# Reordering the loads at the start, moving eight rows of a transform into the prologue, and halving a pair of sums, in a fused Fourier-filter and feed-forward kernel on one core

## The chip, the core and the metric

The kernel runs on one core of a Trainium2 chip. The core has five engines with a program of their own each: TensorE (PE), VectorE (DVE), ScalarE (ACT), GpSimd (POOL) and SyncE (SP). Each takes its instructions strictly in the order written; an instruction that has to wait holds up all that stand behind it on that engine. Transfers between the chip's main memory and the on-chip memories are issued by SP, ACT or POOL and then run on 16 DMA engines that all three share. The metric is the time of one execution on the device, in microseconds (us).

## What is computed

```python
X = np.fft.rfft(x, axis=1)                       # x: 8 batches, 3008 tokens, 256 channels
Y = X * (filt_r + 1j * filt_i)[None, :, :]
y = np.fft.irfft(Y, n=3008, axis=1)
h = y.reshape(24064, 256) @ w_in                 # w_in: 256 x 2048
out = (h - np.tanh(h)) @ w_out                   # w_out: 2048 x 256
```

All inputs and the output are float32 except the weights, which arrive as 64-bit words and are converted to float32 on the core.

## The kernel before

The Fourier transform over 3008 = 64 x 47 tokens is done as matrix products in two stages each way. Tokens are taken in rows r of 47, of which r and 47 - r go together, so that 24 row pairs remain. For each batch there is a *first* stage (a product over the 64 tokens of a row, result to the scratch tensor `ct1`), a middle stage (over the rows, with the filter between there and back, result to the scratch tensor `ct2`), and a *last* stage (`last(i, z)`, from `ct2` through the tile `e2` to the tokens `ut` of a group of four row pairs). A group then goes through the feed-forward part in four units (`up`, `shrink`, `down`).

Batch 0 has to pass the whole transform before anything else can start. This is the **prologue**, some 80 us long: its first stage (`first0`, three chunks of eight rows, tiles `x0`, with the matrix `f0` that VectorE doubles out of the loaded half `fh`), transposes (`across`), the middle stage by seven groups of frequencies (`there0`, `filtered`, `back0`), reads of `ct2` into `e2` (`rest`), and `last(0)`. Where TensorE has nothing to do, `warmer(n)` issues n products whose result nobody reads; each stands as two rows in the trace, since a float32 product is done in two passes.

In the prologue's shadow two other things are done: the weights are converted (`converted`, five VectorE steps for each piece, and sums of pieces, `sums`, which only the later units need), and rows 0 to 7 of batch 1's first stage are computed (`first1`). The rest of batch 1's first stage, and batch 2's, is the generator `first(2, ...)`: one job is four rows of one batch, and jobs are placed between the units of the first groups at positions `due`. The first group's units use a plain form (`up_plain`, L719), the second group's first units already the form with the seven sums (`up`, L648).

The order on each engine is the order in which the code is written (`tc.manual_schedule()`); waits between engines come from the tile framework. Two of its habits matter here. A tile that takes over the space of another waits until everybody has done with the other; so the first tiles of the pool `dn`, opened after the prologue, wait for all users of the prologue's pool `pro` that lie in the same place. And every DMA counts on one of eight semaphores in turn, eight for SP and ACT together and eight for POOL; a DMA waits until the one that had its semaphore before has landed.

Names in the profile: `x`, `fh`, `f` are the tokens and the matrix of the first stage, `pf` its products in PSUM; `ct<-e` are writes of the middle stage's result, `e<-ct` the reads for `last`; `pu` the products of `last`, `odd` the copy of one of its two banks, `ut` the sum and the difference of the two banks; `raw`, `top`, `low`, `wu`, `wd` the steps of converting weights.

Of the kernel before, what the change touches and what calls it, by code (L numbers as in the profile page):

```python
# [9 lines left out]
F32 = mybir.dt.float32  # L10
I32 = mybir.dt.int32
I64 = mybir.dt.int64
# [3 lines left out]
ALU = mybir.AluOpType  # L16
# [101 lines left out]
def kernel(  # L118
# [27 lines left out]
    def dram(t, off, dims):  # L146
        return bass.AP(tensor=t, offset=off, ap=[list(d) for d in dims])
# [112 lines left out]
            for u in dict(after).get(k, ()):  # L260
                yield from sums(u)

    def load_x(t, b, r, n):

        nc.sync.dma_start(t[0:64, 0:n, :], dram(x.tensor, (b * SEQ + r) * DM,
                                                [[NR * DM, 64], [1, n * DM]]))
        lo = 1 if r == 0 else 0
        if lo:
            nc.sync.dma_start(t[64:128, 0, :], dram(x.tensor, b * SEQ * DM,
                                                    [[NR * DM, 64], [1, DM]]))  # L270
        nc.sync.dma_start(t[64:128, lo:n, :], dram(x.tensor, (b * SEQ + NR - r - lo) * DM,
                                                   [[NR * DM, 64], [-DM, n - lo], [1, DM]]))
        return t

    rows = slice(0, 64), slice(64, 128)
# [308 lines left out]
    def last(i, z, held=False):  # L584

        b, c = groups[i]
        n = sum(widths(c))
        e2, gt = e2s.pop(i)
        ut = dn.tile([128, 2, CH * 128], F32, tag="ut", bufs=2, name="ut")
        banks = z("pu", [128, 2, CH, 64])  # L590
        for h in range(2):
            for j, r in enumerate(order(c)):
                for bank, half in zip(banks, rows):
                    for m, part in enumerate(rows):
                        nc.tensor.matmul(bank[part, h, j],  # L595
                                         e2[half, r - CH * c, h * 128 + 64 * m:h * 128 + 64 * m + 64],
                                         gt[half, r - CH * c], start=True, stop=True)
        even, odd = banks
        for k in (1, 0) if held else (1,):
            t = tr.tile([128, 2, CH, 64], F32, tag="e1", bufs=2, name=("even", "odd")[k])  # L600
            ACT.copy(t, banks[k])
            even, odd = (even, t) if k else (t, odd)
        u4 = ut.rearrange("p h (j n) -> p h j n", n=128)
        m = sum(w == 128 for w in widths(c))
        V.tensor_add(u4[:, :, :, 0:64], even, odd)
        V.tensor_sub(u4[:, :, 0:m, 127:63:-1], even[:, :, 0:m], odd[:, :, 0:m])
        w = n // 2
        if i == 0:
            uts[i] = (ut, None, w)
            yield  # L610
            return
# [420 lines left out]
    with tc.tile_pool(name="tr", bufs=2) as tr, tc.manual_schedule():  # L1032
# [16 lines left out]
        with tc.tile_pool(name="pro", bufs=1) as pro, \  # L1049
# [118 lines left out]
            for half in range(2):  # L1168
                V.memset(sgn[64 * half:64 * half + 64], 1.0 - 2 * half)
            V.memset(filt[2][:, 0], 1.0)  # L1170
            xs, began = [], []
            for c in range(3):
                lo = int(c == 0)
                xt = big([128, 8, DM], F32, "x0")
                xs.append(xt)
                fh = pro.tile([128, 8, 64], F32, tag="e1", bufs=4, name="fh")
                (ACT if c else nc.sync).dma_start(fh, f_d[:, 512 * c:512 * c + 512])
                if lo:
                    V.memset(xt[64:128, 0], 0.0)
                for k in (0, 4):  # L1180
                    nc.sync.dma_start(xt[0:64, k:k + 4], dram(x.tensor, (8 * c + k) * DM,
                                                              [[NR * DM, 64], [1, 4 * DM]]))
                    at = max(k, lo)
                    (ACT if c + k == 0 else G).dma_start(
                        xt[64:128, at:k + 4], dram(x.tensor, (NR - 8 * c - at) * DM,
                                                   [[NR * DM, 64], [-DM, k + 4 - at], [1, DM]]))
                r = 8 * c
                V.tensor_copy(f0[:, r:r + 8, 0:64], fh)
                V.tensor_scalar(out=f0[:, r:r + 8, 64:128], in0=fh,
                                scalar1=sgn, scalar2=None, op0=ALU.mult)  # L1190
# [3 lines left out]
            for t in filt:  # L1194
                G.memset(t[0:SG, 2:4], 0.0)
            gate = cst.tile([1, 1], F32, name="gate")
            G.tensor_copy(gate, xs[2][64:65, 0, 0:1])
# [21 lines left out]

            first0(2)  # L1220

            def first1(x1):

                for r in range(0, 8, 2):
                    pf = z0("pf", [128, 2, DM])
                    for k in range(2):
                        nc.tensor.matmul(pf[:, k], f0[:, r + k], x1[:, r + k],
                                         start=True, stop=True)
                    if r % 4 == 0:
                        two = (tr.tile([128, 2, 2, DM], F32, tag="a1", bufs=1, name="a1") if r else  # L1230
                               buffer("xy").rearrange("p (m n) c -> p m n c", m=2))
                    a1 = two[:, r // 2 % 2]
                    ACT.copy(a1, pf)
                    nc.sync.dma_start(
                        dram(ct1[1], r * DM, [[NH * DM, 128], [1, 2 * DM]]), a1)
                    yield

            a2 = {0: across(0)}
            convert(5)
# [68 lines left out]
            next(late)  # L1308
            warmer(8)

        with tc.tile_pool(name="dn", bufs=2) as dn, \
                tc.tile_pool(name="ps", bufs=1, space=bass.MemoryType.PSUM) as ps:
# [57 lines left out]
            for _ in last(0, z2):  # L1370
                pass
            warm = psl([128, 256], "o3")
            for _ in range(4):
                nc.tensor.matmul(warm[0:KM], mats[:, 3 * KM:4 * KM], mats[:, 3 * KM:3 * KM + 256],
                                 start=True, stop=True)
# [147 lines left out]
```

## Time and profile before

| | |
|---|---|
| time, median of 3 runs | 2543.22 us (2541.65 to 2544.98) |
| the profiled execution's own time | 2542.18 us |
| its span in the trace | 2540.3 us |
| busy: PE, DVE, ACT, POOL | 2522.6, 1935.6, 1694.2, 1532.0 us |
| TensorE's granted clock | 0.999 |

Times in the trace are counted from the start of the span. A row of a timeline has the start, the time from the first start to the last end, the engine, the line of the program, what is written and read, the count, and in brackets how long the engine had been idle before and who ended that. "q" behind an engine's name is its sequencer: issuing a DMA, not doing it.

### The profile page before, as it was taken

The page shows a single profiled execution, that of the slowest core. Times are in us where ns is not written, and L with a number is a line of the kernel's source. Part 1 is how long each engine was busy: PE and PEld are TensorE (multiplying, and loading weights), DVE is VectorE, ACT ScalarE, POOL GpSimd, SP SyncE. Part 2 cuts the span into 40 slices and gives each one's busy share as a digit, 9 for nine tenths or more (in the row PEclk, how much of TensorE's full clock was granted, in tenths as well). Part 3 has the DMA queues.
Part 4 walks back from the last instruction along what each step waited for, and adds up shares of the span by engine and source line. Part 5 has one row for each costly group of instructions (what it writes and reads, how often), then busy time and mean ns, then how long its engine had stood idle before and what let it go on. Part 6 is the DMA issues. An engine that isn't in the chain of part 4 may idle for free.

```text
span 2540.3 us, 44575 instructions
## 1 busy us (share of the span) xinstructions
PE 2522.6 (99%) x17072; PEld 2173.1 (86%) x17072; DVE 1935.6 (76%) x2270; ACT 1694.2 (67%) x2551; POOL 1532.0 (60%) x1112
## 2 busy tenths in 40 slices
PE   9999999999999999999999999999999999999998
PEld 8678889888898888988888888898889888898887
DVE  6888877988678876888669886698866888555555
ACT  4666666667666766676667666666666666666665
POOL 5255665667556765676656665666655666455552
PEclk9999999999999999999999999999999999999999
DMA  9854224422343323342334322343123322110110
GB/s 245 261 150 117 65 54 100 112 65 53 86 108 91 82 69 89 80 112 59 80 87 105 87 56 72 96 111 89 36 72 84 92 66 53 26 31 19 25 22 19
DMA packets 333664, 211.37 MB, mean 83 GB/s; under 512 B 231645, under 2 KB 305531, under 8 KB 329793
## 3 DMA queue, kind: packets, MB, share of 16 engines
q1 hardware_dynamic: 319091, 184.93, 29.8%
q0 software_dynamic: 11120, 16.16, 2.3%
q10 hardware_dynamic: 3230, 7.34, 0.9%
q8 instruction: 136, 2.23, 0.4%
q14 instruction: 87, 0.71, 0.1%
HBM read 127.81 MB, written 83.39 MB: 83 GB/s over the span
## 4 chain that ended last, share of the span: by engine, by line
PE 96%; DVE 2%; DMA 1%; issue 0%; POOL 0%; ACT 0%; ACTq 0%; SPq 0%; POOLq 0%; DVEq 0%
PE o L821 44%; PE x L648 25%; PE z L648 12%; PE y L648 6%; PE pm L415 2%; PE pu L595 2%; PE pm L351 1%; PE o L883 1%; PE pf L308 1%; DMA filt<-in_filt_r_dram 1%; DMA x<-in_x_dram 0%; DMA ct<-e 0%; PE o L719 0%; PE x L719 0%; PE z L719 0%
## 5 line engine op out<-in xcount | busy, mean ns | idle before, releaser
L821 PE MATMUL o<-t,wd 128*128 128x256 f32 (+1 forms) x3008 | 762.7, 376 | 0.0
L619 POOL TENSOR_TENSOR t<-h 128x512 f32<-128x512 f32 (+1 forms) x184 | 303.6, 1650 | 707.3 <-DVE h L771 642.2
L771 DVE TENSOR_TENSOR h<-h,y 128x1024 f32<-128x1024 f32 (+1 forms) x384 | 571.0, 1487 | 156.4 <-ACT y L767 156.4
L821 PEld LDWEIGHTS o<-t,wd 128*128 128x128 f32 x3008 | 568.8, 190 | 84.5 <-POOL o L853 15.1
L648 PE MATMUL x<-tu,wu 128*128 128x256 f32 (+1 forms) x2256 | 571.4, 376 | 0.0
L821 PE MATMUL o<-h,wd 128*128 128x256 f32 (+1 forms) x2256 | 569.9, 375 | 0.2 <-DVE h L771 0.2
L648 PEld LDWEIGHTS x<-tu,wu 128*128 128x128 f32 x2256 | 427.4, 190 | 53.8 <-issue 3.9
L821 PEld LDWEIGHTS o<-h,wd 128*128 128x128 f32 x2256 | 428.3, 190 | 50.9 <-issue 0.8
L654 ACT COPY s<-x 128x512 f32<-128x512 f32 (+1 forms) x188 | 109.3, 581 | 517.4 <-PE x L648 517.3
L764 ACT ACTIVATE y<-y 128x1024 f32<-128x1024 f32 (+1 forms) x384 | 399.5, 1040 | 12.1
L767 ACT ACTIVATE y<-y 128x1024 f32<-128x1024 f32 (+1 forms) x384 | 399.8, 1041 | 4.6
L761 ACT ACTIVATE y<-h 128x1024 f32<-128x1024 f32 (+1 forms) x384 | 400.6, 1043 | 2.5 <-DVE h L697 1.7
L622 POOL TENSOR_TENSOR t<-h,t 128x512 f32<-128x512 f32 (+1 forms) x184 | 338.3, 1838 | 0.0
L620 POOL TENSOR_TENSOR t<-h,t 128x512 f32<-128x512 f32 (+1 forms) x184 | 310.5, 1688 | 14.4
L621 POOL TENSOR_TENSOR t<-h 128x512 f32<-128x512 f32 (+1 forms) x184 | 276.9, 1505 | 0.0
L654 ACT COPY u<-x 128x512 f32<-128x512 f32 (+1 forms) x376 | 214.1, 569 | 72.9 <-PE x L648 69.6
L697 DVE COPY h<-x 128x512 f32<-128x512 f32 (+1 forms) x188 | 127.6, 679 | 129.1 <-PE x L648 128.9
L689 DVE TENSOR_TENSOR h<-z,u 128x512 f32<-128x512 f32 (+1 forms) x188 | 127.2, 677 | 88.9 <-ACT u L654 88.5
L648 PE MATMUL x<-ut,wu 128*128 128x256 f32 (+1 forms) x752 | 194.0, 380 | 0.2 <-DVE h L697 0.2
L648 PE MATMUL z<-tu,wu 128*128 128x256 f32 (+1 forms) x752 | 190.2, 375 | 1.4 <-DVE h L705 1.4
L648 PE MATMUL y<-ut,wu 128*128 128x256 f32 (+1 forms) x752 | 190.1, 375 | 0.0
L648 PE MATMUL z<-ut,wu 128*128 128x256 f32 (+1 forms) x752 | 190.0, 375 | 0.0
(215 smaller groups left out, 2933.5 us busy)
## 6 DMA issues: line engine op xcount, KB each, us to landing
ft<-filt SPq DMA_DIRECT2D x28, 1024.0 KB
ct<-nn SPq DMA_DIRECT2D x56, 512.0 KB
e<-ct SPq DMA_DIRECT2D x47, 512.0 KB
a<-ct SPq DMA_DIRECT2D x112, 192.0 KB
out_dram<-ot SPq DMA_DIRECT2D x1248, 16.0 KB
x_sb<-in_x_dram SPq DMA_DIRECT2D x110, 128.0 KB
ct<-a SPq DMA_DIRECT2D x60, 128.0 KB
ct<-x_sb SPq DMA_DIRECT2D x60, 128.0 KB
```

Of the source, the lines that this page charges most:

```text
L619: by.tensor_sub(t[0], b[0][1], b[0][0])
L620: by.tensor_sub(t[1], b[1][1], t[0])
L621: by.tensor_sub(t[2], b[1][1], b[0][1])
L622: by.tensor_sub(t[3], b[1][0], t[1])
L648: nc.tensor.matmul(bank[:, k], wu[:, q - 1, (2 * u + k) * 128:(2 * u + k + 1) * 128], rhs[q - 1], start=(first and k == 0), stop=True, ski ...
L654: ACT.copy(t, X)
L697: V.tensor_copy(h[:, 2, :, 0:w], X)
L761: ACT.activation(y[k], ht[k], AF.Arctan, scale=TURN)
L764: ACT.activation(y[k], y[k], AF.Tanh, scale=BEND)
L767: ACT.activation(y[k], y[k], AF.Square, scale=SCALE, accum_out=y_sums[:, 2 * U + k // 2:2 * U + k // 2 + 1])
L771: V.tensor_mul(ht[k], ht[k], y[k])
L821: nc.tensor.matmul(product(q), wd[:, q - 1, (2 * u + k) * 128: (2 * u + k + 1) * 128], rhs[q - 1][:, k], start=(u == 0 and k == 0 and q == ...
```

## The change

Seven edits, in the order of the program.

1. The chunks of `x0` and `f` are issued in another order and from other queues. The first half of `f`'s first chunk goes ahead on SP; ACT carries the first chunk's upper tokens, the other half of that `f`, and then both later chunks of `f`; POOL carries the upper tokens of chunks 1 and 2 alone, and behind its memsets. `f0` is doubled in pieces of 4, 4, 8 and 8 rows. POOL's filter loads wait for the last of the upper tokens.
2. `warmer(15)` at the start becomes `warmer(8)`.
3. Rows 8 to 15 of batch 1's first stage leave `first(2, ...)` (two jobs fewer there) and come into the prologue, as a second `first1` with a tile `x1b`, which POOL loads. Its results go through two tiles that take the places of `raw` in the pool `pro`.
4. The results of both `first1` are written to `ct1` from POOL, 512 KB at a time, where SP wrote 256 KB at a time.
5. The reads of `ct2` for `last(0)`: those of the first five groups go to POOL's queue (`rest` of 25 rows), those of the last two (7 rows) to SP and ACT. The final conversions of the prologue and `first1` stand ahead of the latter.
6. `warmer(8)` at the end of the prologue becomes `warmer(2)`, and four products behind `last(0)` become two.
7. `last(0)` copies, adds and subtracts the two halves of its channels one after the other, where one operation took both.

```diff
@@ last(i, z)
+        if i == 0:
+            t = tr.tile([128, 2, CH, 64], F32, tag="e1", bufs=2, name="odd")
+            for h in range(2):
+                ACT.copy(t[:, h], odd[:, h])
+                V.tensor_add(u4[:, h, :, 0:64], even[:, h], t[:, h])
+                V.tensor_sub(u4[:, h, 0:m, 127:63:-1], even[:, h, 0:m], t[:, h, 0:m])
...
@@ the prologue's loads
-            for c in range(3):
-                (ACT if c else nc.sync).dma_start(fh, f_d[:, 512 * c:512 * c + 512])
-                for k in (0, 4):
-                    nc.sync.dma_start(xt[0:64, k:k + 4], ...
-                    (ACT if c + k == 0 else G).dma_start(xt[64:128, at:k + 4], ...
...
+            load_f(0, 0, 4, nc.sync)
+            load_high(0, 0, ACT)
+            load_low(0, 0, nc.sync)
+            load_f(0, 4, 4, ACT)
+            load_high(0, 4, ACT)
+            load_low(0, 4, nc.sync)
+            for c in (1, 2):
+                load_f(c, 0, 8, ACT)
+            for c in (1, 2):
+                for k in (0, 4):
+                    load_low(c, k, nc.sync)
+                    load_high(c, k, G)
+            for c, k, n in ((0, 0, 4), (0, 4, 4), (1, 0, 8), (2, 0, 8)):
+                doubled(c, k, n)
...
-            G.tensor_copy(gate, xs[2][64:65, 0, 0:1])
+            G.tensor_copy(gate, xs[2][64:65, 4, 0:1])
-            warmer(15, filt[2][:, 0])
+            warmer(8, filt[2][:, 0])
...
@@ first1
-            def first1(x1):
+            def first1(x1, at, tiles):
-                    ACT.copy(a1, pf)
-                    nc.sync.dma_start(
-                        dram(ct1[1], r * DM, [[NH * DM, 128], [1, 2 * DM]]), a1)
+                    ACT.copy(two[:, r // 2 % 2], pf)
+                    if r % 4:
+                        G.dma_start(dram(ct1[1], (r - 2) * DM, [[NH * DM, 128], [1, 4 * DM]]),
+                                    two.rearrange("p m n c -> p (m n c)"))
+            def raw_tile():
+                t = pro.tile([128, 512], I64, tag="raw", bufs=3, name="a1")
...
@@ the prologue's end
+                    x1b = load_x(big([128, 8, DM], F32, "x1b"), 1, 8, 8, G)
...
-            rest(0, SG * (last_g - 1), [nc.sync])
+            rest(0, SG * (last_g - 1), [G])
             way_back()
-            rest(SG * (last_g - 1), NA - SG * (last_g - 1), [nc.sync])
-            fs = first(2, z2, [(1, c) for c in range(2, NX)])
+            convert(100)
+            first1(x1, 0, [...])
+            rest(SG * (last_g - 1), NA - SG * (last_g - 1), [nc.sync, ACT])
+            fs = first(2, z2, [(1, c) for c in range(4, NX)])
             next(fs)
-            convert(100)
-            for _ in first1(x1):
-                pass
+            first1(x1b, 8, [raw_tile, raw_tile])
...
-            warmer(8)
+            warmer(2)
...
-            for _ in range(4):
+            for _ in range(2):
                 nc.tensor.matmul(warm[0:KM], ...
-            due = [4 + (LEAD - 4) * k / (NX + 4) for k in range(NX + 4)]
+            due = [4 + (LEAD - 4) * k / (NX + 2) for k in range(NX + 2)]
```

ScalarE at the start of the program, before and after: `x` is the first chunk's upper tokens (three rows, the fourth is not loaded), `fh` pieces of the matrix.

```order
L1184 DMA x_87<-in_x_dram 64x3x256
L1177 DMA fh<-f 128x512 x2
L1193 ACT_TABLE_LOAD
L1193 ACTIVATE warm_b<-warm_b 128x1
L1074 COPY wd<-pf 128x256x2 x8
```

```order
L1188 DMA x_87<-in_x_dram 64x3x256
L1193 DMA fh<-f 128x256
L1188 DMA x_87<-in_x_dram 64x4x256
L1193 DMA fh<-f 128x512 x2
L1218 ACT_TABLE_LOAD
L1218 ACTIVATE warm_b<-warm_b 128x1
L1079 COPY wd<-pf 128x256x2 x8
```

The second and third chunks of the matrix (`128x512`) stand behind two more transfers in ACT's queue.

ScalarE at the end of the prologue, before and after: from the last write of `ct2` over the copies of `first1` (`xy`, `a`) to `last(0)` (`odd`).

```order
L483 DMA ct_0<-e_615 48x2x128
L181 ACTIVATE top<-raws 128x512
L1233 COPY xy<-pf 128x512 x2
L1233 COPY a_665<-pf 128x512 x2
L601 COPY odd<-pu 128x512
```

```order
L483 DMA ct_0<-e_614 48x2x128
L181 ACTIVATE top<-raws 128x512
L1254 COPY xy<-pf 128x512 x2
L1254 COPY a_651<-pf 128x512 x2
L1134 DMA e_448<-ct_0 7x1024 x2
L1254 COPY a_673<-pf 128x512 x2
L1254 COPY a_683<-pf 128x512 x2
L604 COPY odd<-pu 128x256 x2
```

ACT now issues two of the reads of `ct2`, and the copies of the second `first1` stand behind them.

GpSimd from the load of `x1b` on, after, with the semaphores that each row waits for (before, only the loads of weights stood there).

```order
L265 DMA x1b<-in_x_dram 64x2048 [waits DMAHW3_49,DMAHW2_49,DMASW1_49]
L271 DMA x1b<-in_x_dram 64x8x256 [waits DMASW2_49]
L175 DMA a_68<-in_moe_w_out_dram 128x2x256 [waits DMASW3_49,PE_49]
L175 DMA a_68<-in_moe_w_in_dram 128x2x256 [waits DMASW4_49,PE_49,Activation_49]
L1134 DMA e_448<-ct_0 25x1024 [waits DMAHW6_49,DMAHW0_49,DMASW5_49]
L1134 DMA e_448<-ct_0 25x1024 [waits DMAHW7_49,DMAHW1_49,DMASW6_49]
L1134 DMA e_448<-ct_0 25x1024 [waits DMASW7_49]
L1134 DMA e_448<-ct_0 25x1024 [waits DMASW0_49]
L1256 DMA ct_1<-xy 128x1024 [waits DMASW1_49,DVE_49,Activation_49]
L1256 DMA ct_1<-a_651 128x1024 [waits DMASW2_49,Activation_49]
L1256 DMA ct_1<-a_673 128x1024 [waits DMASW3_49,Activation_49]
L1256 DMA ct_1<-a_683 128x1024 [waits DMASW4_49,Activation_49]
```

Ten transfers (the first two rows, the four reads `e<-ct` and the four writes to `ct1`) stand on POOL that were not there before, eight of them between the loads of weights. Since the eight semaphores are taken in turn, the last write, of `a_683`, counts on the one called `DMASW4_49`, the write of `a_673` on `DMASW3_49`.

VectorE at `last(0)`, after: the end of the prologue's conversions, the four operations on halves, and the next conversion.

```order
L201 TENSOR_TENSOR wu<-top,low 128x2x256 [waits DVE_49]
L605 TENSOR_TENSOR ut<-pu,odd 128x4x64 [waits DMASW6_49,DMASW5_49,DMAHW0_49,DMASW4_49,DMAHW1_49,DMASW3_49,DMAHW2_49,DMASW2_49,DMAHW3_49,DMASW1_49,DMAHW6_49,DMASW0_49,DMAHW7_49,DVE_49,Activation_49]
L606 TENSOR_TENSOR ut<-pu,odd 128x3x64
L605 TENSOR_TENSOR ut<-pu,odd 128x4x64 [waits Activation_49]
L606 TENSOR_TENSOR ut<-pu,odd 128x3x64
L183 TENSOR_SCALAR xy<-xy 128x512 [waits Activation_49]
```

The first operation on `ut` waits for `DMASW4_49` and `DMASW3_49`: `ut` takes space that the tiles `a_673` and `a_683` had, so it waits until both have been written to `ct1`. Before, it waited only for writes of `ct2` out of that space.

More of the change, by code (lines that the diff above doesn't have):

```diff
@@ L598, in last @@
         even, odd = banks
+        u4 = ut.rearrange("p h (j n) -> p h j n", n=128)
+        m = sum(w == 128 for w in widths(c))
+        if i == 0:
[4 more added lines that the diff above has]
+                V.tensor_sub(u4[:, h, 0:m, 127:63:-1], even[:, h, 0:m], t[:, h, 0:m])
+            uts[i] = (ut, None, n // 2)
+            yield
+            return
         for k in (1, 0) if held else (1,):
@@ L1170 @@
             V.memset(filt[2][:, 0], 1.0)
-            xs, began = [], []
-            for c in range(3):
[L1173 to L1176, printed above, removed]
-                (ACT if c else nc.sync).dma_start(fh, f_d[:, 512 * c:512 * c + 512])
-                if lo:
-                    V.memset(xt[64:128, 0], 0.0)
-                for k in (0, 4):
[L1181 to L1190, printed above, removed]
+            xs, began = [big([128, 8, DM], F32, "x0") for _ in range(3)], []
@@ new lines, with load_low, load_high @@
+            fhs = [pro.tile([128, 8, 64], F32, tag="e1", bufs=4, name="fh") for _ in range(3)]
+            V.memset(xs[0][64:128, 0], 0.0)
+            for t in filt:
+                G.memset(t[0:SG, 2:4], 0.0)
+            def load_low(c, k, queue):
+                queue.dma_start(xs[c][0:64, k:k + 4], dram(x.tensor, (8 * c + k) * DM,
+                                                           [[NR * DM, 64], [1, 4 * DM]]))
+            def load_high(c, k, queue):
+                at = max(k, int(c == 0))
+                queue.dma_start(xs[c][64:128, at:k + 4],
+                                dram(x.tensor, (NR - 8 * c - at) * DM,
+                                     [[NR * DM, 64], [-DM, k + 4 - at], [1, DM]]))
@@ new lines, in load_f, with doubled @@
+            def load_f(c, k, n, queue):
+                queue.dma_start(fhs[c][:, k:k + n],
+                                f_d[:, 512 * c + 64 * k:512 * c + 64 * (k + n)])
+            def doubled(c, k, n):
+                r, half = 8 * c + k, fhs[c][:, k:k + n]
+                V.tensor_copy(f0[:, r:r + n, 0:64], half)
+                V.tensor_scalar(out=f0[:, r:r + n, 64:128], in0=half,
+                                scalar1=sgn, scalar2=None, op0=ALU.mult)
+            load_f(0, 0, 4, nc.sync)
@@ L1220 @@
             first0(2)
-            def first1(x1):
-                for r in range(0, 8, 2):
+            def first1(x1, at, tiles):
+                for r in range(at, at + 8, 2):
                     pf = z0("pf", [128, 2, DM])
                     for k in range(2):
-                        nc.tensor.matmul(pf[:, k], f0[:, r + k], x1[:, r + k],
+                        nc.tensor.matmul(pf[:, k], f0[:, r + k], x1[:, r + k - at],
                                          start=True, stop=True)
                     if r % 4 == 0:
[L1230 to L1233, printed above, removed]
-                    nc.sync.dma_start(
-                        dram(ct1[1], r * DM, [[NH * DM, 128], [1, 2 * DM]]), a1)
-                    yield
+                        two = tiles.pop(0)()
+                    ACT.copy(two[:, r // 2 % 2], pf)
[4 more added lines that the diff above has]
+                t = pro.tile([128, 512], I64, tag="raw", bufs=3, name="a1")
+                return t.bitcast(F32).rearrange("p (m n c) -> p m n c", m=2, n=2)
             a2 = {0: across(0)}
@@ L1297 @@
                     ahead = [begun(tiles1, job, queue=G) for job in jobs[5:7]]
[L1298 removed]
+            rest(0, SG * (last_g - 1), [G])
             way_back()
[L1300 to L1301 removed]
+            convert(100)
+            first1(x1, 0, [lambda: buffer("xy").rearrange("p (m n) c -> p m n c", m=2),
+                           lambda: tr.tile([128, 2, 2, DM], F32, tag="a1", bufs=1, name="a1")])
+            rest(SG * (last_g - 1), NA - SG * (last_g - 1), [nc.sync, ACT])
+            fs = first(2, z2, [(1, c) for c in range(4, NX)])
             next(fs)
[L1303 to L1305 removed]
+            first1(x1b, 8, [raw_tile, raw_tile])
             late = weights(tiles1, jobs[5:], G, ahead, 4,
```

22 lines of the change are left out of this document (7 added, 15 removed).

## The prediction

> **What bounds the kernel now.** I read the busy times first, then TensorE's timeline over the first 80 us, then its waits, and last what stands before each wait.
>
> ```profile
> PE 2522.6 (99%) x17072; PEld 2173.1 (86%) x17072; DVE 1935.6 (76%) x2270; ACT 1694.2 (67%) x2551; POOL 1532.0 (60%) x1112
> ...
> 0.00:20.00 20.00, 18.55 (x114) 16.95 (x115) 3.84 (x12) 7.90 (x11) 10.00 (x21) 1.00 0.94 240
> 20.00:66.00 46.00, 42.93 (x234) 36.13 (x233) 40.64 (x61) 21.90 (x39) 21.91 (x29) 1.00 0.88 251
> 66.00:80.00 14.00, 11.24 (x112) 9.32 (x111) 10.90 (x21) 5.12 (x10) 0.00 (x0) 1.00 0.59 164
> 80.00:142.00 62.00, 61.84 (x261) 37.99 (x261) 57.63 (x113) 42.59 (x70) 21.54 (x28) 1.00 0.92 278
> ```
>
> The last four lines give for a stretch the busy time of PE, its weight loads, DVE, ACT and POOL, then the clock, the DMA engines' share and GB/s. TensorE is busy all the time, so an edit counts only where it takes products away or closes a gap, and all of that lies in the first 142 us. Behind TensorE stands VectorE: between 80 and 142 us it is busy for 57.63 of 62 us.
>
> ```profile
> 1.45 9.44 PE L1081 MATMUL warm<-filt 120*128 120x256 f32 x30 [1.45 <-DVE filt L1170]
> ...
> 8.78 2.10 PE L1081 MATMUL warm<-filt 120*128 120x256 f32 x9
> 10.72 10.88 PE L1071 MATMUL pf<-f,x 128*128 128x128 f32 x96
> ...
> 65.67 1.04 PE L478 MATMUL pe<-xy,mats_sb 112*112 112x128 f32 x8
> 66.55 3.62 PE L1227 MATMUL pf<-x,f 128*128 128x256 f32 x16
> 70.00 3.62 PE L1081 MATMUL warm<-f 128*128 128x256 f32 x16
> 76.05 0.33 PE L595 MATMUL pu<-gt,e 64*64 64x64 f32 x4 [2.42 <-DMA e<-ct]
> 76.71 1.15 PE L595 MATMUL pu<-gt,e 64*64 64x64 f32 x60 [0.34 <-issue]
> 77.79 1.99 PE L1374 MATMUL pt<-mats_sb 120*120 120x256 f32 x8
> 79.77 1.77 PE L719 MATMUL x<-ut,wu 128*128 128x448 f32 x4
> ...
> 141.79 1.13 PE L648 MATMUL x<-ut,wu 128*128 128x256 f32 x4 [0.17 <-DVE h L697]
> ```
>
> Filling products stand at the start (30 rows), at 70.00 (16) and at 77.79 (8); the only long wait is the 2.42 us for `e`. At 141.79 TensorE waits for VectorE, which until then is level with it.
>
> **The first stage of batch 0 (edits 1, 2).** Of 30 filling rows 14 go. They are late ones: nine take 2.10 us, so 14 take about 3.1 and TensorE is free at 7.8 instead of 10.9. The first four rows' data should be there; then the matrix decides.
>
> ```profile
> 11.10 0.43 DVE L1188 COPY f<-fh 128x512 f32<-128x512 f32 x1 [5.54 <-DMA fh<-f]
> 11.44 0.48 DVE L1189 TENSOR_SCALAR f<-fh,sgn 128x512 f32<-128x512 f32 x1
> 15.12 0.43 DVE L1188 COPY f<-fh 128x512 f32<-128x512 f32 x1 [3.20 <-DMA fh<-f]
> ...
> 4.55 1.93 POOL L1195 MEMSET filt<- 5x512 f32 x3
> 15.40 0.19 POOL L1197 COPY gate<-x 1x1 f32<-1x1 f32 x1 [8.91 <-DMA x<-in_x_dram]
> ```
>
> VectorE waited for the second chunk of `f` until 11.10 and for the third until 15.12: a chunk of 256 KB took 4.02 us on ACT's queue beside two busy queues. Now 384 KB more stand ahead of both there. By that price they would come 6.0 us later, at 17.1; at the other end POOL, which starts 1.93 us later and carries 256 KB less, leaves so much room that they come no later than now. I take 2.5 us, nearer to the low end since small pieces go ahead while POOL is still silent: 13.6. Doubling takes 0.8 us (11.10 to 11.92), then 64 of the 96 rows of 10.88 us are left: 13.6 + 0.8 + 7.25 = 21.7, against 10.72 + 10.88 = 21.6 now. The reorder only trades a wait on fillers for a wait on `f`: **+0.1** (from -2.0, if the chunks come when they do now, where the third one's 15.12 + 0.8 + 3.6 = 19.6 decides, to +3.6). POOL's filters wait for a later load than at 15.40, by a microsecond or two; VectorE's other work covers that, I take nothing. Rows 20 to 66 are unchanged and move with this.
>
> **The end of the prologue (edits 3 to 7), in the times of before.** TensorE: the second `first1` costs another 3.62 us and takes the place of six of eight fillers (2.7), done at 74.5, still before `e` is there; hidden. What counts is on ACT, POOL and VectorE.
>
> ```profile
> 69.80 1.06 ACT L1233 COPY xy<-pf 128x512 f32<-128x512 f32 x2
> 70.74 1.09 ACT L1233 COPY a<-pf 128x512 f32<-128x512 f32 x2
> ...
> 73.28 1.36 SPq L1129 DMA_DIRECT2D e<-ct  x4
> ...
> ft<-in_moe_w_in_dram POOLq DMA_DIRECT2D x1, 512.0 KB, 6.5
> ft<-in_moe_w_out_dram POOLq DMA_DIRECT2D x1, 512.0 KB, 7.7
> ...
> ct<-e POOLq DMA_DIRECT2D x6, 240.0 KB, 5.1
> ...
> 78.56 0.69 DVE L605 TENSOR_TENSOR ut<-pu,odd 128x512 f32<-128x512 f32 x1 [2.58 <-DMA x_sb<-in_x_dram]
> ...
> 125.30 0.41 DVE L229 TENSOR_TENSOR wu<-wu 128x256 f32<-128x256 f32 x1
> ```
>
> SP issued the last reads at 73.28, when the last writes of `ct2` had landed. ACT now issues two of them itself and cannot go on before: 73.3, plus 2 x 0.34 = 74.0. Only then come its copies of the second `first1`, four in 2.03 us as from 69.80 to 71.83: 76.0. Behind ACT wait TensorE's `pu` (76.05 as now; reads from two queues save the 0.34 us and no more) and POOL, which issues the last write to `ct1`. The third number of a DMA line is the time from issue to landing: 6.5 to 7.7 us for 512 KB from POOL, 5.1 for 240 KB. I take 6.5: the write has landed at 82.5. VectorE's first operation on `ut` waits for it, since `ut` lies where the written tile lay; it stood at 78.56. Behind it on VectorE stand all conversions. Then an addition and a subtraction on a half (0.41 each): TensorE's first product of the feed-forward part starts at 83.3 instead of 79.77, **+3.6**. The ends: no earlier than a landing at 74.1 (TensorE's products done at 73.5 and a copy) + 5.1 = 79.2, +0.3; no later than the whole traffic takes, POOL's four writes of 512 KB and SP's 1.3 MB from 74.0 at 278 GB/s, 86, +7.1. Halving the sums and two fillers fewer (1.0 us) save nothing while TensorE waits.
>
> The Trainium skill's page "DMA: Bandwidth & Descriptors" (Anatomy of one DMA) fits a POOL transfer by 2.0 us plus its bytes at 436 GB/s, an estimate of 3.2 us for 512 KB; the landing would be at 79.2, the term +0.3, the sum, with no stop of the clock, -0.8. The measured 6.5 us decides.
>
> TensorE then idles from 78.2 to 83.3. After 2.42 us of idling its rows cost no more (1.99 us for eight at 77.79); after the idle before the program the 30 rows cost 9.44 us, though 16 later ones cost 3.62, so 30 would cost 6.8: 2.6 lost. Five microseconds lie between; I take **+1.7** (0 to 2.6).
>
> The Trainium skill's page "TensorE: Matmul & The Clock Gate" (Part 1: The HAM clock gate) says that after an idle window of some 3.4 us the array runs at half rate for another such window, which would be 1.7 us; no run here shows it in the middle of a program.
>
> **Two jobs fewer (edit 3).**
>
> ```profile
> 83.67 0.43 DVE L183 TENSOR_SCALAR xy<-xy 128x512 f32<-128x512 f32 x1 [0.52 <-ACT xy L181]
> ...
> 92.93 1.09 DVE L771 TENSOR_TENSOR h<-h,y 128x896 f32<-128x896 f32 x1 [0.69 <-ACT y L767]
> ...
> 97.15 0.43 DVE L183 TENSOR_SCALAR xy<-xy 128x512 f32<-128x512 f32 x1 [0.61 <-ACT xy L181]
> ...
> 106.03 1.09 DVE L771 TENSOR_TENSOR h<-h,y 128x896 f32<-128x896 f32 x1 [0.37 <-ACT y L767]
> ...
> 122.17 0.69 DVE L605 TENSOR_TENSOR ut<-pu,odd 128x512 f32<-128x512 f32 x1 [0.22 <-ACT odd L601]
> ...
> 85.89 1.89 PE L308 MATMUL pf<-x_sb,f 128*128 128x256 f32 x8
> 87.61 1.67 PE L719 MATMUL x<-ut,wu 128*128 128x448 f32 x4
> ```
>
> A job takes TensorE 1.72 us (85.89 to 87.61), two 3.4. But at 141.79 TensorE waits for VectorE, whose work is the same as before and which idled little on the way. The idle pieces at 97.15, 106.03 and 122.17 can shrink with earlier products and a freer ACT, 1.2 us together; those at 83.67 and 92.93 lie before any job has been saved. So **-1.2**, with 0 and -3.4 as ends.
>
> **Sum:** 0.1 + 3.6 + 1.7 - 1.2 = +4.2 on the profiled execution's own 2542.2, that is 2546.4. The median of the runs shown stood 1.0 above it: 2547.4, say 2547.5.
>
> **Rivals.** *POOL's queue is later still* (0.27): the write of `a_683` is the last of four in that queue, beside SP's loads, and lands at 86. For it: the 278 GB/s that all queues together reach. Against: loads of that size landed in 7.7 us at most in a busier stretch. Term +7.1 for +3.6, sum +7.7: 2551. It decides from a landing at 83.4 on. *POOL is early* (0.14): ACT is free sooner and the write takes 5.1 us; term +0.3, no long idle, sum 0.1 + 0.3 - 1.2 = -0.8: 2542.4. *VectorE is not the bound* (0.09): the two jobs count in full, sum 0.1 + 3.6 + 1.7 - 3.4 = +2.0: 2545.2. *All goes as written* (0.07): -2.0 + 0.3 - 3.4 = -5.1, and a shorter gap at `e` besides: 2538 or less.
>
> **Chances.** The forecast has 0.43, with a range of its own from 2544.5 to 2550.5. The bound for "same", 0.2% or 5.1 us, is about what a measurement of this kernel can tell from no change; it ends at 2548.3, inside that range: I give 0.26 of the 0.43 to "same", 0.17 to "slower". With the rivals: faster 0.07; same 0.26 + 0.14 + 0.09 = 0.49; slower 0.17 + 0.27 = 0.44. The range leaves out the last rival and the far end of the first: 2540.5 to 2553.
>
> **What would show it.** In the changed profile: VectorE waits for `fh` until about 13.6 and the first stage ends near 21.7; ACT idles up to about 73.3 for a write of `ct2`; the first `ut` waits for a DMA `ct<-a` until about 82.5, and TensorE idles some 5 us before `x` of the plain units; rows behind that idle are slow; later there is a wait of one to three microseconds for VectorE near 140. I am wrong if `ut` starts before 80, if `f` comes by 12, or if the first stage ends after 24.

## The result, and the profile after

| | median, us | lowest to highest | ratio to before, 95% interval |
|---|---|---|---|
| before | 2541.65 (5 runs) | 2541.0 to 2544.98 | |
| after | 2556.32 (5 runs) | 2554.26 to 2562.33 | 1.0059 [1.0047, 1.0070] |

The change costs 14.7 us; 2547.5 with 2540.5 to 2553 was forecast. The profiled execution took 2559.28 us, 17.1 above that of before and 3.0 above the median of its five.

First TensorE's waits in the changed kernel: who waited for whom, us in total, how often, the longest.

```profile
PE pu L595 <- DMA e<-ct: 7.3, 2, 4.9
PE pf L1076 <- issue: 4.9, 1, 4.9
PE x L724 <- DVE ut L606: 2.5, 1, 2.5
PE z L653 <- DVE h L694: 1.5, 1, 1.5
```

Of these, only the waits for `ut` and for `h` were forecast. The 4.9 us in the first stage and the second wait for `e` are new. TensorE's timeline shows where they stand.

```profile
7.91 1.95 PE L1076 MATMUL pf<-f,x 128*128 128x128 f32 x16
14.76 10.52 PE L1076 MATMUL pf<-f,x 128*128 128x128 f32 x80 [4.90 <-issue]
...
69.91 1.10 PE L478 MATMUL pe<-xy,mats_sb 112*112 112x128 f32 x8 [0.38 <-DVE xy L458]
...
85.94 0.48 PE L595 MATMUL pu<-gt,e 64*64 64x64 f32 x4 [4.91 <-DMA e<-ct]
88.80 1.97 PE L595 MATMUL pu<-gt,e 64*64 64x64 f32 x60 [2.38 <-DMA e<-ct]
...
95.25 2.55 PE L724 MATMUL x<-ut,wu 128*128 128x448 f32 x4 [2.49 <-DVE ut L606]
...
103.06 1.89 PE L308 MATMUL pf<-x_sb,f 128*128 128x256 f32 x8
...
155.95 1.13 PE L653 MATMUL z<-ut,wu 128*128 128x256 f32 x4 [1.46 <-DVE h L694]
157.68 2.08 PE L653 MATMUL x<-ut,wu 128*128 128x256 f32 x4 [0.60 <-DVE h L702]
159.54 1.73 PE L653 MATMUL y<-ut,wu 128*128 128x256 f32 x4
161.11 1.67 PE L888 MATMUL o<-h,wd 128*128 128x448 f32 x4
```

In the profile before, the row that answers to the last of these is:

```profile
143.62 1.67 PE L883 MATMUL o<-h,wd 128*128 128x448 f32 x4
```

Set against the same rows of before, the delay grows in five steps. The first stage ends at 14.76 + 10.52 = 25.28 instead of 21.60: +3.7; at L478, the last products of the middle stage, it is 69.91 - 65.67 = +4.2. The first feed-forward product (`x`) starts at 95.25 instead of 79.77: +15.5, so 11.2 more come from the end of the prologue. From `x` to the first `pf` of a job it takes 7.81 us instead of 6.12: the rows at a lower clock (granted 0.50 from 96.2 to 99.4 us), +1.7. Two jobs fewer take back 3.4, but at 155.95 and 157.68 TensorE waits 2.1 us for VectorE, and the rows behind that are slow again: 157.68 to 161.11 is 3.43 us where 141.79 to 143.62 was 1.83, +1.6, at a granted clock of 0.50 to 0.55. These last 1.6 us seem to belong to this execution rather than to the change: in the profiles of back_only and own_space below the same two waits stand at this place (1.49 and 0.60 us, 1.26 and 0.60), and the rows behind them run at a granted clock of 1.00.

The other engines show where this comes from. The first two rows are VectorE's waits for `f`, in the first stage. The rest is about the 11.2 us: the next row is ScalarE's longest wait for a buffer of `e` before the change, the one behind it the same after; then come SP, GpSimd (its last write to `ct1`: issue, and the time to landing) and VectorE at the end of the prologue.

```profile
16.87 0.43 DVE L1198 COPY f<-fh 128x512 f32<-128x512 f32 x1 [9.71 <-DMA fh<-f]
18.35 0.43 DVE L1198 COPY f<-fh 128x512 f32<-128x512 f32 x1 [0.66 <-DMA fh<-f]
```

```profile
66.12 0.59 ACT L1144 COPY e<-pe 120x512 f32<-120x512 f32 x1 [1.35 <-DMA ct<-e]
```

```profile
73.13 0.59 ACT L1149 COPY e<-pe 120x512 f32<-120x512 f32 x1 [6.39 <-DMA ct<-e]
...
81.95 0.65 SPq L1134 DMA_DIRECT2D e<-ct  x2
...
85.64 0.53 POOL L1256 DMA_DIRECT2D ct<-a  x1 [0.45 <-ACT a L1254]
...
ct<-a POOLq DMA_DIRECT2D x1, 512.0 KB, 8.3
...
94.51 0.42 DVE L605 TENSOR_TENSOR ut<-pu,odd 128x256 f32<-128x256 f32 x1 [11.57 <-DMA gt<-g]
```

ScalarE stood 6.39 us before it could write a tile `e`, because earlier writes of `ct2` out of it had not landed; before, that wait was 1.35. So the last reads of `ct2` went out 12.0 us after L478 instead of 7.6: **+4.4**. From there to the second group of `pu` it took 88.80 - 81.95 = 6.9 us instead of 76.71 - 73.28 = 3.4: **+3.4**. From that group to `x` it took 6.5 instead of 3.1: **+3.4**, nearly all of it VectorE's wait before `ut`. The profile names `gt<-g` for that wait, but on the semaphore of that transfer the instruction needs only an earlier count. The last write to `ct1` is among the counts it needs: issued at 85.64 on GpSimd, 8.3 us to landing, so 93.9.

Why were the writes of `ct2` slow? The queues from 66 to 72 us, after: q0 is GpSimd's, q1 SP's; packets, MB, share of time.

```profile
q0 software_dynamic: 327, 1.24, 79.9%
q1 hardware_dynamic: 319, 0.31, 21.6%
```

Both sent as many packets, but GpSimd's (loads of `x1b` and of weights) held 3.8 KB each and SP's (writes of `ct2`) 1 KB: four fifths of the time went to loads nobody was waiting for. The Trainium skill's page "DMA: Bandwidth & Descriptors" (Queues, rings and completion order) says that a DMA engine takes its queues in turn, a packet at a time; these counts agree. Counts were not equal in every run, though (304 against 791 in the same window of high_pool below), so the rule alone gives no price.

### The profile page after: what moved, and what is told of

It is laid out like the page before. It is cut to its first block, busy times and chain, and to the rows that moved or that the text cites. A ratio compares the mean times of both kernels' runs of the same rounds, so it can differ in the third digit from the quotient of the medians.

```text
span 2557.4 us, 44512 instructions
## 1 busy us (share of the span) xinstructions
PE 2524.1 (99%) x17042; PEld 2171.9 (85%) x17042; DVE 1936.6 (76%) x2274; ACT 1694.4 (66%) x2552; POOL 1537.3 (60%) x1121
## 4 chain that ended last, share of the span: by engine, by line
PE 96%; DMA 1%; DVE 1%; issue 1%; ACT 0%; POOL 0%; ACTq 0%; SPq 0%; DVEq 0%; POOLq 0%
PE o L826 44%; PE x L653 25%; PE z L653 12%; PE y L653 6%; PE pm L415 2%; PE pu L595 2%; PE pm L351 1%; DMA ct<-e 1%; PE o L888 1%; PE pf L308 1%; PE pf L1076 0%; PE o L724 0%; DMA gt<-g 0%; PE x L724 0%; PE z L724 0%
```

## The experiments

All medians in the table are beside runs of before on the same chip. The intervals of the slower ones overlap; what tells them apart is the place of a wait in the profile.

| variant | median, us | before, us | ratio, 95% interval | start of `x`, us |
|---|---|---|---|---|
| front_only | 2547.19 | 2542.10 | 1.0017 [1.0007, 1.0026] | 86.40 |
| back_only | 2555.52 | 2542.10 | 1.0056 [1.0042, 1.0070] | 92.89 |
| high_pool | 2557.36 | 2542.10 | 1.0057 [1.0043, 1.0071] | 94.77 |
| no_x1b | 2552.78 | 2542.10 | 1.0048 [1.0035, 1.0062] | 88.80 |
| own_space | 2553.71 | 2543.19 | 1.0046 [1.0033, 1.0060] | 92.39 |
| fillers | 2556.42 | 2543.19 | 1.0053 [1.0040, 1.0067] | 94.80 |
| no_second | 2553.69 | 2543.72 | 1.0044 [1.0030, 1.0058] | 90.96 |
| no_both | 2547.63 | 2543.72 | 1.0018 [1.0009, 1.0027] | 85.58 |
| load_only | 2548.40 | 2543.23 | 1.0020 [1.0011, 1.0029] | 87.97 |
| fewer_jobs | 2542.53 | 2543.19 | 0.9996 [0.9987, 1.0005] | 81.10 |
| short_start | 2543.28 | 2543.19 | 1.0003 [0.9994, 1.0012] | 80.25 |
| late_weights | 2544.96 | 2543.72 | 1.0005 [0.9996, 1.0014] | 81.64 |

### The two halves of the change: front_only and back_only

The first is before with edits 1 and 2 (from `xs, began =` to `warmer(8)`), the second is after with those lines of before.

> Before, with the change's edits 1 and 2 alone. Theory (the four upper rows of the first chunk now ride in ACT's queue in 1 KB packets and land at about 14.7 us; TensorE's rows 4 to 7 wait for them): the first stage ends near 25.3 instead of 21.6, all behind it moves by that, total +3.7 us, about 2545.4. Rival (the 2.4 us wait for e at the end of the prologue, or VectorE behind it, swallows the delay): the first stage ends late all the same, but the total stays within 1.5 us of before.

> After, with the loads and fillers at the start as before: edits 3 to 7 alone. Theory (the two parts add up): first stage ends at 21.6, the first product of the feed-forward part starts near 91.5, total +11 us, about 2552.7. Rival (the slow writes of ct2 at the end come from the late start, which pushes POOL's loads into them): the prologue's end is hardly later than before, first product at 83 or less, total +3 to +5, about 2546.

TensorE in front_only, then in back_only:

```profile
13.96 3.34 PE L1071 MATMUL pf<-f,x 128*128 128x128 f32 x16 [3.99 <-issue]
17.79 7.42 PE L1071 MATMUL pf<-f,x 128*128 128x128 f32 x64 [0.48 <-DVE f L1194]
...
27.98 2.00 PE L428 MATMUL pa<-a,mats_sb 120*120 120x256 f32 x4 [0.79 <-DVE a L1099]
```

```profile
71.60 2.02 PE L478 MATMUL pe<-xy,mats_sb 112*112 112x128 f32 x8 [5.66 <-DVE xy L458]
...
92.89 3.22 PE L724 MATMUL x<-ut,wu 128*128 128x448 f32 x4 [2.68 <-DVE ut L606]
```

The new start alone costs 5.1 us, a little more than forecast: the first stage ends at 25.21, and behind two short gaps some rows run at half clock (granted 0.51 from 28.0 to 31.5 us). The rest alone costs 13.4. Together that would be 18.5, where both cost 14.7; the intervals leave some 5 us open, so the totals do not show that the parts fail to add up. The profile shows more. In back_only L478 comes at 71.60, later than in the whole change (69.91), although the first stage ended 3.6 us sooner; VectorE, and TensorE behind it, waited for transfers (VectorE 7.55 us for the last filters, where it had waited 1.51 before). So when the second part is in, an early or a late start makes little difference.

### The late rows at the start: high_pool

```diff
-            load_high(0, 4, ACT)
+            load_high(0, 4, G)
```

> After, with one load moved: the first chunk's upper rows 4 to 7 go first on POOL's queue instead of third on ACT's. Theory (queues share the DMA engines by packets, so 1 KB packets on ACT get a quarter of the bytes; POOL's packets are 4 KB): these rows land at about 9 us, TensorE does not stop for 4.9 us, the first stage ends at 20.5 to 21.5, the total is 4 us below the changed kernel, 2552. Rival (all queues together are the limit, so another piece comes late instead): the first stage still ends after 24, total 2555 to 2557.

The packets of the three queues from 7 to 15 us (q10 is ScalarE's), after and then high_pool, and TensorE and a row of VectorE in high_pool:

```profile
q1 hardware_dynamic: 263, 0.87, 40.4%
q0 software_dynamic: 226, 0.73, 33.3%
q10 hardware_dynamic: 423, 0.58, 31.2%
```

```profile
q0 software_dynamic: 281, 0.95, 45.8%
q1 hardware_dynamic: 268, 0.90, 42.2%
q10 hardware_dynamic: 174, 0.30, 15.3%
```

```profile
9.67 0.43 DVE L1198 COPY f<-fh 128x512 f32<-128x512 f32 x1 [1.85 <-DMA fh<-f]
...
10.24 2.02 PE L1076 MATMUL pf<-f,x 128*128 128x128 f32 x16 [0.29 <-issue]
...
15.21 5.88 PE L1076 MATMUL pf<-f,x 128*128 128x128 f32 x48 [0.31 <-DMA x<-in_x_dram]
...
73.68 2.02 PE L478 MATMUL pe<-xy,mats_sb 112*112 112x128 f32 x8 [4.11 <-DVE xy L458]
...
94.77 3.35 PE L724 MATMUL x<-ut,wu 128*128 128x448 f32 x4 [5.73 <-DVE ut L606]
```

Where ScalarE's queue carried these rows it sent the most packets and the fewest bytes. With them on GpSimd's queue the stop of 4.9 us is gone and the first stage ends at 21.09, as expected, and the total is not lower at all: both theories were wrong. The run does not tell the rows from the matrix: with 256 KB less ahead of them, the later chunks of `f` came at 9.67 and 14.65 too, where they had come at 16.87 and 18.35. L478 comes at 73.68, since VectorE waited 5.04 and 5.33 us for filters, and `x` half a microsecond earlier than in the whole change. The gain at the start is used up by these later waits for transfers.

### The extra transfers: no_x1b, no_second, no_both, load_only

```diff
 no_x1b (after)
-                    x1b = load_x(big([128, 8, DM], F32, "x1b"), 1, 8, 8, G)
+                    x1b = x1
 no_second (after; later jobs write other rows in their place)
-            first1(x1b, 8, [raw_tile, raw_tile])
 no_both: no_second, and without the load of x1b
 load_only (before)
+                    load_on_pool(big([128, 8, DM], F32, "x1b"), 1, 8, 8)
                     ahead += [begun(tiles1, job, queue=G) for job in jobs[7:9]]
```

> After, without the load of x1b (1 MB on POOL's queue): the second first1 takes the rows of the first one, so that rows 8 to 15 of batch 1's first stage are wrong. Theory (POOL's large packets hold back the writes of ct2, in 1 KB packets on SP): POOL's queue is empty 4.6 us earlier, ACT's wait of 6.4 us for a buffer of e shrinks to under 2 us, the last reads of ct2 are issued at about 77.5 instead of 81.95, total 4.4 us below the changed kernel, 2552. Rival (the loads of weights alone hold them back, or the writes are slow by themselves): last reads still after 81, total 2555 to 2557.

> After, without the second first1: no products, copies and writes of it, but x1b is still loaded (its rows of ct1 get other rows, written by the two jobs behind them, so that part of batch 1 is wrong). Theory (up to the first feed-forward product the queues move 233 to 246 GB/s whatever the kernel, so its start follows the bytes in front of it: 22.84 MB at 95.25 us in the changed kernel): 1 MB less, x at about 91, no wait of ut for a write to ct1, total 4 us below the changed kernel, 2552. Rival (the load of x1b alone makes the delay, the writes to ct1 are hidden): x at 94 or later, total 2555 to 2557.

> The same without the load of x1b as well: of the moved rows nothing is left in the prologue. Theory (bytes): 2 MB less than the changed kernel, x at 86.5, as with the new start alone (86.40), total 2546 to 2547. Rival (the four writes to ct1 from POOL in 512 KB pieces, the reads on POOL and ACT and the halves cost by themselves): x at 89 or later, total over 2549.

> Before, with one thing added: the load of x1b (1 MB, which nothing reads) on POOL's queue ahead of the last two loads of weights, where the change has it. Theory (its large packets hold back the writes of ct2 and the filters on SP's queue in 1 KB packets): ScalarE waits 4 us or more for a buffer of e where it waited 1.35, the last reads of ct2 are issued at 77 to 78.5 instead of 73.28, x of the plain units near 84.5 instead of 79.77, total +5 us, ratio about 1.002. Rival (the gaps of the queues at the end of the prologue, 0.59 busy from 66 to 80 us, take the extra megabyte): last reads before 75, total within 1.5 us of before.

ScalarE and SP in no_x1b; TensorE and SP in load_only:

```profile
68.16 0.59 ACT L1149 COPY e<-pe 120x512 f32<-120x512 f32 x1 [1.26 <-DMA ct<-e]
...
75.56 0.65 SPq L1134 DMA_DIRECT2D e<-ct  x2
```

```profile
72.05 2.02 PE L484 MATMUL pe<-xy,mats_sb 112*112 112x128 f32 x8 [5.75 <-DVE xy L464]
...
81.51 1.37 SPq L1135 DMA_DIRECT2D e<-ct  x4
...
87.97 1.77 PE L725 MATMUL x<-ut,wu 128*128 128x448 f32 x4
```

Without the load, ScalarE's wait falls from 6.39 to 1.26 and the last reads go out at 75.56 instead of 81.95, earlier even than expected. The load alone, added to before with nobody reading it, moves these reads from 73.28 to 81.51 and costs 5.2 us, as forecast, though the reads and `x` (87.97) came some 3 us later in the profile than forecast: this is the clearest of all the runs, since nothing else differs. It came in part by another way than expected, since VectorE too waited for its filters, so L478 is 6.4 us late. no_second starts `x` at 90.96 and no_both, without anything of the moved rows, is where front_only is, both as expected. From no_both over no_second to after, the ratios rise from 1.0018 to 1.0044 to 1.0059: the new start, with the reads on other queues, costs some 4.6 us, the load 6.6, and the second `first1` with its writes 3.8, the first uncertain by 2 us and the others by 4 to 5. The last is not clear of noise by the totals alone; what speaks for it is the start of `x`, 95.25 against 90.96.

What the queues had moved by the start of `x`, in before (0 to 79.8 us), no_both (85.6), no_second (91) and after (95.25):

```profile
DMA packets 10951, 18.63 MB, mean 233 GB/s; under 512 B 1737, under 2 KB 7266, under 8 KB 10880
```

```profile
DMA packets 11960, 20.00 MB, mean 234 GB/s; under 512 B 1878, under 2 KB 8203, under 8 KB 11889
```

```profile
DMA packets 12150, 21.02 MB, mean 231 GB/s; under 512 B 1906, under 2 KB 8202, under 8 KB 12015
```

```profile
DMA packets 12790, 22.85 MB, mean 240 GB/s; under 512 B 1978, under 2 KB 8388, under 8 KB 12655
```

In these four the time goes with the bytes, at 231 to 240 GB/s. That is not a law: front_only and load_only reached only 219 and 224, front_only starts `x` 6.6 us later than before with 0.36 MB more, and a later `x` lets in loads of later work. So the bytes alone do not give the start of `x`; what the runs above do show is that transfers delay it, although TensorE is shown busy for 72.5 of the 79.8 us before (fillers included).

### The wait before ut: own_space

```diff
-            first1(x1, 0, [lambda: buffer("xy").rearrange(...), lambda: tr.tile(... "a1")])
+            kept_xy = buffer("xy").rearrange("p (m n) c -> p m n c", m=2)
+            first1(x1, 0, [lambda: kept_xy, lambda: tr.tile(... "a1")])
-            first1(x1b, 8, [raw_tile, raw_tile])
+            first1(x1b, 8, [lambda: kept_xy, lambda: tr.tile(... "a1")])
```

> After, with the results of the second first1 in the two tiles outside the prologue's pool that the first one used (they wait there for its writes to land), so that no later tile takes their space. Theory (ut waits for the last write to ct1, landed at 93.9 us): the first ut stands directly behind its copy, near 91.5 instead of 94.51, x of the plain units near 92.3 instead of 95.25, total 3 us below the changed kernel, 2553.3. Rival (transfers as a whole are the limit, something else is waited for there instead, or ScalarE's wait for the reused tiles delays the copy): x still after 94, total 2555 to 2557.

VectorE and TensorE in own_space:

```profile
91.09 0.42 DVE L605 TENSOR_TENSOR ut<-pu,odd 128x256 f32<-128x256 f32 x1 [9.07 <-ACT odd L604]
...
92.39 2.01 PE L724 MATMUL x<-ut,wu 128*128 128x448 f32 x4
```

`ut` now waits for its copy and nothing else, `x` starts 2.9 us earlier, and the median is 2.6 below the changed kernel's, though the intervals of the two ratios overlap. ScalarE now stood 5.32 us for the write of a tile that it reuses, which the rival had named, and `x` came earlier all the same. The predicted chain from ScalarE over the write to `ct1` to `ut` was there.

### The clock and VectorE: fillers, fewer_jobs

```diff
 fillers (after)
-            warmer(2)
+            warmer(14)
-            for _ in range(2):
+            for _ in range(10):
 fewer_jobs (before; later jobs write other rows in place of those left out)
-            fs = first(2, z2, [(1, c) for c in range(2, NX)])
+            fs = first(2, z2, [(1, c) for c in range(4, NX)])
...
```

> After, with 14 filling products instead of 2 at the end of the prologue and 10 instead of 2 behind last, about 5 and 4 us of them, in TensorE's idle time. Theory (the clock stays up, but VectorE, late by the whole delay, is the bound up to 155 us): the rows behind the wait run at full speed (1.67 us for four rows of x instead of 2.55), TensorE gets there 2 us earlier and waits 2 us longer for VectorE near 155, total unchanged within 1 us of the changed kernel. Rival (the slow rows lie on the path): total 1.9 us less, 2554.4.

> Before, with the two jobs for rows 8 to 15 of batch 1 left out of the units (their place in ct1 gets other rows, written by the two jobs after them, so that part of batch 1 is wrong) and nothing in their place. Theory (VectorE is the bound up to 142 us): TensorE has 3.4 us less to do but waits 1.8 to 3.4 us for VectorE there, total -1.2 us, 2540.9, at least 2540.0. Rival (TensorE is the bound): -3.4 us, 2538.7.

TensorE in fillers, then in fewer_jobs:

```profile
94.80 2.77 PE L724 MATMUL x<-ut,wu 128*128 128x448 f32 x4 [2.39 <-DVE ut L606]
```

```profile
141.08 1.83 PE L649 MATMUL z<-ut,wu 128*128 128x256 f32 x4 [2.52 <-DVE h L690]
142.81 2.07 PE L649 MATMUL x<-ut,wu 128*128 128x256 f32 x4
```

The fillers settled nothing: 2.39 us of idling were left, and the rows behind them were slow all the same (granted clock 0.57 from 95 to 99 us). The total did not change, and the waits for VectorE near 155, forecast 2 us longer, were 0.7 us shorter. fewer_jobs did settle its question: of 3.4 us less work 0.7 came out (interval -3.3 to +1.3), as the products of 141.08 wait 2.52 us for VectorE, and the rows behind that wait are slow. VectorE is the bound up to there.

### A better version: short_start, late_weights

```diff
 short_start (before, with last(0) by halves as in the change)
-            warmer(15, filt[2][:, 0])
+            warmer(8, filt[2][:, 0])
-            for _ in range(4):
+            for _ in range(2):
 late_weights: short_start, and in it
-                    ahead += [begun(tiles1, job, queue=G) for job in jobs[7:9]]
...
             way_back()
+            ahead += [begun(tiles1, job, queue=ACT) for job in jobs[7:9]]
```

> Before, with 8 filling products at the start instead of 15, the sums of last(0) by halves and 2 fillers behind it instead of 4; loads as before. Theory (with the old order the pieces land in step with the products): first stage ends at 20.2 instead of 21.6, x of the plain units at 77.7 instead of 79.8, total -1.5 to -2, 2540.3. Rival (transfers set the end of the prologue): the first stage ends earlier, the wait for e grows by as much, x at 79 or later, total within 0.8 us of before.

> Before, with the short start (8 fillers, halves, 2 fillers behind last), and the two 512 KB loads of weights that ran on POOL's queue from 56 to 65 us, beside the writes of ct2, issued by ScalarE behind the last write of ct2. Theory (these loads hold back the writes of ct2 and the loads of filters; without them the earlier first stage gets through): ScalarE's wait of 2.8 us for a buffer of e is gone, pu at 73.5 to 74.5 instead of 75.8, x at 78 instead of 80.25, total 2541, 1 to 2.5 us below before. Rival (the way from the last write of ct2 to the reads is one of latencies, not of bytes, or the weights now come late for VectorE): x at 79.5 or later, total within 0.8 us of before or above.

TensorE in short_start, and VectorE in late_weights:

```profile
12.22 7.38 PE L1076 MATMUL pf<-f,x 128*128 128x128 f32 x64 [0.20 <-DMA x<-in_x_dram]
...
75.81 0.48 PE L595 MATMUL pu<-gt,e 64*64 64x64 f32 x4 [3.00 <-DMA e<-ct]
```

```profile
60.57 0.69 DVE L452 TENSOR_TENSOR xy<-xy,filt 120x512 f32<-120x512 f32 x1 [4.21 <-DMA filt<-in_filt_i_dram]
```

With the old order of loads the first stage ends at 19.6, 2 us before that of before, and nothing comes of it: `pu` starts 0.2 us earlier, the wait for `e` is longer, the time is the same. Moving the two loads of weights out of the way took away ScalarE's wait for a buffer of `e` (2.81 us in short_start), as expected, and did not help either: VectorE's wait for a filter, which comes on SP's queue, was 4.21 us instead of 3.22. No version was found that beats before.

## Why the prediction was wrong, step by step

- **The first stage, +0.1 forecast, +3.7 measured.** The term that was mis-sized is the landing of `f`. The prediction's own price made the second chunk 6.0 us later, and it took 2.5 of them, "nearer to the low end", so 13.6; the chunk came at 16.87, 5.8 us later. By the prediction's sum that alone gives 16.87 + 0.8 + 7.25 = 24.9, so +3.3, and its sign of being wrong, an end after 24, was there (25.28). One thing was overlooked besides: "the first four rows' data should be there; then the matrix decides" looked at rows 0 to 3 and at `f`, not at rows 4 to 7, whose upper tokens now stood third in ScalarE's queue, and TensorE stood until 14.76. But with the same start and these rows earlier, TensorE stood for `f` instead: own_space went on at 12.93 and fillers at 11.89, both then waited for `f` (until 17.76 and 16.99), and their first stages ended at 26.8 and 26.0, rows behind the wait being in part at half clock. TensorE in own_space:

```profile
17.76 9.04 PE L1076 MATMUL pf<-f,x 128*128 128x128 f32 x64 [2.81 <-DVE f L1199]
```

- **The writes of `ct2`, nothing forecast, +4.4.** "In the times of before" took over the landing at 73.3 as it stood. The load of `x1b`, 1 MB on GpSimd's queue, had no price in the sum. This is the term that was missing, and it is the largest: 5.2 us added to before, 6.6 between no_both and no_second. Without it, in no_x1b, the reads went out 6.0 us after L478, where it took 7.6 before and 12.0 after.
- **The last reads, "save the 0.34 us and no more", +3.4.** That they could be slower beside the writes to `ct1` was not considered. From the issue on SP to the second group of `pu` it took 5.9 us in no_second and 5.4 in no_both, which lack the writes of the second `first1`, against 3.4 in load_only and 3.6 in front_only. So at least 2 of the 3.4 us come without those writes, with the other edits at this place: the reads on two queues, or the first `first1`'s writes, which now leave GpSimd ahead of the reads. Which of these it is was not tried and stays open.
- **The write to `ct1` and `ut`, right in mechanism.** Wait, place and chain are as forecast; the write took 8.3 us where 6.5 was taken. Only the reason was misread: in the built program `ut` lies at byte 137,856 of each partition and the two tiles at 193,664 and 201,856, 4 KB each, so `ut` does not lie where they lay. It waits because its pool takes over from the prologue's. Since the rest was late too, taking it away gains 2.9 us at `x`.
- **The clock, +1.7 forecast, +1.7 measured** behind the wait. That the size fits is partly luck: the forecast had five microseconds of idling before `x`, and it was 2.49, about the 2.42 that cost nothing before. But TensorE had stood 4.91 and 2.38 us for `e` shortly ahead of it, and its clock was at 0.50 from 82.5 to 92.7 already. A second slow stretch at 157.68, +1.6, was not foreseen; other runs with the same waits there do not have it.
- **Two jobs fewer, -1.2 forecast.** Here -3.4 + 2.1 = -1.3, and -0.7 in fewer_jobs. Right, as far as these runs can tell.
- **The rivals.** None held a late `e`. All of them, like the forecast, took TensorE's and ScalarE's order as the frame and put transfers in singly, each with the time it took in before.

## What to carry to other kernels

Work that is moved to fill TensorE's gaps takes its transfers along: count their bytes, and look whether the queues have room for them over the whole stretch (here their share was 0.84 of the time, at 233 GB/s, up to the first feed-forward product). A look at the last part alone misleads: 0.59 from 66 to 80 us before, and the load still cost 5.2 us. A transfer that nobody waits for has a price when one that somebody waits for runs beside it; that small packets make it worse is argued from the packet counts and was not tried. Making an engine earlier at the beginning of a stretch can be used up by longer waits for transfers later in it, as in short_start and high_pool.

## What was not expected of the hardware

- Gaps far shorter than the five microseconds reckoned with can lower TensorE's clock: 1.46 and 0.60 us of idling in after (rows behind at 157.68 take 1.86 us for four instead of 0.97, granted clock 0.50), 0.93 and 0.79 in front_only (from 27.98 to 31.49 about twice the usual time). The same gaps can also cost nothing: 0.94 and 0.78 in after (granted clock 1.00 from 28.0 to 31.5), 1.49 and 0.60 in back_only. The prediction quotes an idle window of some 3.4 us; the gaps that cost something are shorter, and the measurement decides. The Trainium skill's page "TensorE: Matmul & The Clock Gate" (Part 1: The HAM clock gate) says that the window in which activity is judged runs freely and does not start anew with the kernel. If so, the place of a gap in the window can matter; that like gaps have two outcomes agrees, and no run here tries it.
- A megabyte that nothing reads costs 5.2 us (interval 2.8 to 7.4), about the 4.5 us that its 1.05 MB take at the 233 GB/s of the queues' mean: it was not hidden, although TensorE is shown busy nearly all the time.
